# Differences in the comparison of the transform matrices: GpSimd in place of VectorE

## The chip, the cores and the metric

The kernel runs on one core of a Trainium2 chip. Its engines each work through a list of their own: TensorE (PE; PEld is its loading of weights), VectorE (DVE), ScalarE (ACT), GpSimd (POOL) and SyncE (SP), which here issues the transfers (DMA). They meet at semaphores only. The metric is the device time of one execution in microseconds (us). The time before is a median of 1157.23 us over three runs (1155.76 to 1159.63).

## What is computed

The reference adds two branches to its input, both fed by the same layer norm (S = 2048 rows, D = 512):

```python
xn = layernorm(x)
# A: Fourier mixing with the transform matrices given as inputs
a = xn @ dft_hid_re.T;  b = xn @ dft_hid_im.T
A = dft_seq_re @ a - dft_seq_im @ b
# B: product-key experts: 32 heads, 64 x 64 keys, 4096 experts, top 2 each
q1, q2 = split(xn @ w_q);  s1, s2 = q1 @ k1.T, q2 @ k2.T
top_s, top_e = top2(top2(s1) + top2(s2));  g = softmax(top_s)
B = sum(g * gelu(xn . u[top_e]) * v[top_e])
out = x + A + B
```

The transform matrices are inputs, not constants. They normally have the symmetries of a Fourier transform: columns that are mirrored, or equal up to a sign. The kernel computes branch A from a part of each matrix, using these symmetries. So that the result holds for any input, it also reads the matrices as a whole and measures how far they are from the symmetries. A flag at the end selects a general branch where they are not; with these inputs it isn't taken.

## The kernel before, in words

**Stages.** Up to about 480 us the kernel normalizes, computes branch A by folded matrices, and routes branch B (scores, top values, indices). The rest, from about 480 us to the end, is the expert stage in `part_b`. It walks over 16 blocks of 128 rows. For a block b it has

- a **z phase**: for all 4096 experts, z = u . xn, by `u_part` (L975, 12 matmuls per group of 128 experts). ScalarE takes z from PSUM through gelu into the tile act (L982). Two blocks share a phase for most of the kernel, with z groups in four PSUM banks in turn.
- **g products** (`g_mm`): the routing weights as a dense matrix. VectorE builds one-hot matrices L (L1003) and R (L1008, then times the gate in L1011) for 16 rows at a time, in three buffers; TensorE multiplies them into PSUM (L1013), two halves of 16 rows per call.
- **w parts** (`w_part`): VectorE multiplies act by g (L1021, g is read from PSUM), ScalarE rounds it to f16 (L1028; VectorE does so in L1026 in the z phases), VectorE forms the remainder (L1029). Four parts make the block's left-hand side, in place in the act tile (which is called act or w in the trace).
- a **v phase**: `v_part` multiplies by v (L1058, 96 matmuls of 512 columns). Of 16 tiles of v nine stay in SBUF; seven are streamed from DRAM by SP (L1049), three buffers.
- `add_x` loads y (branch A's result) and x and adds them on GpSimd (L1071); `finish` adds the v sum (L1075) and stores (L1076).

The phases run z(2,3), v1, v2, z(4,5), v3, v4 and so on. So a v block with an odd number is followed by an even one, for which the last w part is made during the odd block; an even v block is followed by a z phase. While v of the even block runs, the g products and first w parts of the following odd block are made.

**The comparison.** 64 units `compare(n)` (L1080 to L1134) and four `compare_w(n)` measure the symmetries. A dictionary `plan` names after which group of a phase a unit is emitted: three units in each v block up to 13, at groups 4, 5 and 6, and five in each double z phase. A unit n takes a tile cx of 128 x 1024 f32 (four slots of 256 columns): the first 128 columns come with one transfer (L1087), the other 896 with another (L1088). Then

1. L1089 (VectorE) sums the absolute values of the first 128 columns.
2. Where g is 1, 2 or 3 (48 units), L1108 subtracts slot 0 from, or adds it to, the slots 1 to 3, in one instruction of 768 columns or in two of 512 and 256. Where g is 0 (16 units), slot 1 is done by L1095, slots 2 and 3 by two L1097 with a factor of 0 for partition 0, and L1099 does partition 0 of slot 3.
3. `mirror` (L1114, for kk = 0 also L1116) subtracts or adds mirrored halves, for the whole tile in slot 0, and where g is 0 for partition 0 in slot 2. L1128 adds a constant on partition 0 in four units; L1122, L1125, L1130 and L1133 set some entries to others or to zero.
4. ScalarE sums the absolute values of all that is left (L1134). This is put on the list `later`, so that it is emitted about two units later.

The tile cx comes from the pool tag "w" with four buffers (WB = 4), the same that the w parts use and that `fit` (sums over other weights, L1186, L1193, L1197) loads into.

**What sets the order.** The code is emitted in the order of the plan. A scheduler in the framework then makes one list for each engine when the program is built: it takes instructions by priority, with an estimate of its own of when their inputs are there, and places the waits. So the engine on which an instruction runs can shift the order of others on VectorE and ScalarE. Once built, the lists are fixed, and each engine works strictly in order.

Of the kernel before, what the change touches and what calls it, by code (L numbers as in the profile page):

```python
# [15 lines left out]
ALU = mybir.AluOpType  # L16
AX = mybir.AxisListType

P = 128
# [15 lines left out]
def tile_fnet_peer(ctx, tc, x, ca, cb, c5, wt, wf, wr, wq, kt, ut, vn, out):  # L35
# [9 lines left out]
    nc = tc.nc  # L45
# [494 lines left out]
    c52 = cst.tile([1, 2], F32, name="c52")  # L540
# [122 lines left out]
    def part_b(safe, stS, stP, stE, xt, u_sb, cmp_p, w4):  # L663
# [416 lines left out]
        def compare(n):  # L1080

            ri, g, kk = n // 32, n // 8 % 4, n % 8
            odd = kk // 4
            t = bp.tile([P, 4, 4, 64], F32, tag="w", name=f"cx{n}", bufs=WB)
            tf = t.rearrange("p s q c -> p (s q c)")
            tv = t.rearrange("p s q c -> p s (q c)")
            nc.sync.dma_start(tf[:, :P], ca[ri, g, :, kk * P:(kk + 1) * P])  # L1087
            nc.sync.dma_start(tf[:, P:], cb[ri, g, kk].rearrange("p b c -> p (b c)"))  # L1088
            nc.vector.tensor_reduce(asum[:, n:n + 1], tf[:, :P], axis=AX.X, op=ALU.add,  # L1089
                                    apply_absolute_value=True)  # L1090
            sgn = (((1, 1, 1), (-1, 1, -1)), ((-1, -1, 1), (1, -1, -1)))[ri][odd]
            ops = [ALU.subtract if v > 0 else ALU.add for v in sgn]
            op = ops[1]
            if g == 0:
                nc.vector.tensor_tensor(tv[:, 1], tv[:, 1], tv[:, 0], op=ops[0])  # L1095
                for i in (2, 3):
                    nc.vector.scalar_tensor_tensor(tv[:, i], tv[:, 0], not0, tv[:, i], op0=ALU.mult, op1=ops[i - 1])  # L1097
                f = (-1 if ri else 1) * sgn[1] * sgn[2]
                nc.vector.tensor_tensor(tv[0:1, 3], tv[0:1, 3], tv[0:1, 2],  # L1099
                                        op=ALU.subtract if f > 0 else ALU.add)  # L1100
            else:
                sets = {}
                for i, o in enumerate(ops):
                    sets.setdefault(o, []).append(i + 1)
                for o, ix in sets.items():
                    sl = slice(ix[0], ix[-1] + 1, ix[1] - ix[0] if len(ix) > 1 else 1)
                    v = tv[:, sl]
                    nc.vector.tensor_tensor(v, v, tv[:, 0:1].to_broadcast([P, len(ix), 256]), op=o)  # L1108
            m = ALU.add if ri else ALU.subtract

            def mirror(v):

                c = 0 if kk else 1
                nc.vector.tensor_tensor(v[:, 2:4, c:], v[:, 2:4, c:], v[:, 0:2, c:], op=m)  # L1114
                if c:
                    nc.vector.tensor_tensor(v[:, 3, 0:1], v[:, 3, 0:1], v[:, 2, 0:1], op=m)  # L1116

            if g == 0:
                mirror(t[0:1, 2])
                if odd and ri:  # L1120

                    nc.vector.tensor_copy(t[0:1, 2, 0:2], t[0:1, 0, 0:2])  # L1122
                elif odd == ri:
                    if ri:
                        nc.vector.memset(t[0:1, 2, 0:2], 0.0)  # L1125
                    else:
                        v = t[0:1, 2, 0:2].rearrange("p q (c a) -> p (q c) a", a=2)
                        nc.vector.tensor_tensor(v, v, c52.unsqueeze(1).to_broadcast([1, 64, 2]), op=ALU.add)  # L1128
                    if kk == 0:
                        nc.vector.memset(t[0:1, 2, 2, 0:1], 0.0)  # L1130
            mirror(t[:, 0])
            if kk == 0:
                nc.vector.memset(t[:, 0, 2, 0:1], 0.0)  # L1133
            later.append(lambda: nc.scalar.activation(tf[:, P:], tf[:, P:], AF.Abs, accum_out=chk[:, n:n + 1]))  # L1134
# [248 lines left out]
    with tc.If(rv > 0):  # L1383
        with tc.tile_pool(name="gen", bufs=1) as gp, \
# [10 lines left out]
            def gload(src, shape, tag, name):  # L1395
                t = gp.tile(shape, F32, tag=tag, name=name, bufs=2)
                nc.sync.dma_start(t, src)
                return t
# [6 lines left out]
            for q in range(4):  # L1405
                ya = gp.tile([P, 4, D], F32, tag="ya", name=f"gya{q}")
                for ri in range(2):
# [25 lines left out]
                    for a in range(4):  # L1433
# [12 lines left out]
                        o = gload(out[b * P:(b + 1) * P], [P, D], "o", f"go{b}")  # L1446
# [54 lines left out]
```

## Time and profile before

| | |
|---|---|
| median of three runs | 1157.23 us (1155.76 to 1159.63) |
| the profiled execution | 1159.15 us, its span 1157.3 us |
| TensorE busy | 1131.3 us (98%), mean granted clock 0.99 |
| VectorE busy | 930.0 us (80%) |
| ScalarE busy | 608.5 us (53%) |
| GpSimd busy | 256.3 us (22%), most of it before 480 us |
| DMA | 167.82 MB, mean 145 GB/s |
| comparisons | L1108 runs from 568.9 to 1018.4 us, L1114 from 501.0 to 1019.1 us |

How to read it: all rows of the profile are of one execution, in us from the start of its span. A group row names line, engine, operation, output tile <- input tiles, shapes and count; then busy time in us and the mean duration in ns; then the idle time of the engine just before these instructions and what ended it ("<-DMA cx" is a transfer into cx, "<-PE g L1013" a TensorE instruction). A row of waits has the total, the number and the longest wait. A row of the timeline has start, duration, engine and line. Matmuls are pipelined, so that the duration of one is longer than its share of the engine's time. GpSimd's spans are rough.

### The profile page before, as it was taken

The numbers are of one execution on the slowest core, as the hardware profiler recorded it, in microseconds if no ns is written. First come the engines' busy times: TensorE is split into PE (matmuls) and PEld (weight loads), VectorE is DVE, ScalarE is ACT, GpSimd is POOL, SyncE is SP. The second block draws the span as 40 slices with busy tenths as digits, with TensorE's granted clock in tenths as the row PEclk, the third lists the DMA queues.
The fourth block names the chain that finished last, engine by engine and source line by source line (L and its number), as shares of the span: only waits on it lengthen the run. The fifth ranks groups of instructions, "written<-read, shape, count | busy, mean of one in ns | idle before, by whom it ended". The sixth has DMA issues, their size and how long they took to land.

```text
span 1157.3 us, 25208 instructions
## 1 busy us (share of the span) xinstructions
PE 1131.3 (98%) x9862; PEld 719.8 (62%) x9862; DVE 930.0 (80%) x2846; ACT 608.5 (53%) x1045; POOL 256.3 (22%) x226
## 2 busy tenths in 40 slices
PE   5999899999999999999999999999999999999997
PEld 4445455445445459778478479569569559658763
DVE  7979789799898998974994895897886886788670
ACT  7765487686786735354435435535535436433440
POOL 2371464865865411000000000010010000000000
PEclk9998899999999999999999999999999999999999
DMA  9992345243241204261743743654555555452423
GB/s 344 229 254 90 129 132 176 63 163 128 74 164 47 83 15 125 84 213 38 245 148 105 233 163 107 220 162 137 185 159 174 169 172 168 156 167 63 138 75 104
DMA packets 98335, 167.82 MB, mean 145 GB/s; under 512 B 32916, under 2 KB 48155, under 8 KB 98206
## 3 DMA queue, kind: packets, MB, share of 16 engines
q1 hardware_dynamic: 97904, 166.04, 44.5%
q8 instruction: 79, 1.29, 0.5%
q14 instruction: 50, 0.41, 0.1%
q10 hardware_dynamic: 302, 0.08, 0.0%
HBM read 142.69 MB, written 17.63 MB: 139 GB/s over the span
## 4 chain that ended last, share of the span: by engine, by line
PE 63%; DVE 21%; POOL 7%; issue 3%; ACT 3%; DMA 2%; SPq 0%; POOLq 0%; DVEq 0%; ACTq 0%
PE v L1058 28%; PE z L975 26%; DVE vals L841 5%; PE s L245 5%; DVE idx L845 4%; PE g L1013 4%; POOL w L153 2%; POOL w L154 2%; POOL u L722 1%; DVE z L782 1%; DVE L L1003 1%; DVE m L220 1%; DVE ft L406 1%; DVE z L783 1%; DVE u L510 1%
## 5 line engine op out<-in xcount | busy, mean ns | idle before, releaser
L975 PE MATMUL z<-xb,u 128*128 128x256 f16 (+1 forms) x3840 | 342.7, 251 | 0.2 <-ACT w L982 0.2
L975 PEld LDWEIGHTS <-u 128*128 128x128 f16 x3840 | 309.7, 98 | 26.7 <-issue 0.3
L245 PE MATMUL s<-m,xq 128*128 128x512 f16 x1344 | 301.4, 383 | 0.0
L1058 PE MATMUL v<-v,act 128*128 128x512 f16 x1056 | 233.2, 379 | 0.0
L245 PEld LDWEIGHTS <-xq 128*128 128x128 f16 x1344 | 131.0, 99 | 155.0 <-issue 7.0
L1003 DVE TENSOR_TENSOR L<-io_lam,cmp 128x2048 f16<-128x2048 f16 x128 | 156.0, 1219 | 62.2 <-PE g L1013 62.1
L1058 PEld LDWEIGHTS <-act 128*128 128x128 f16 x1056 | 101.3, 98 | 117.6
L1071 POOL TENSOR_TENSOR y<-y,xr 128x512 f32<-128x512 f32 x15 | 28.1, 1874 | 612.9 <-DMA y<-y_d 393.1
L841 DVE MAX8 vals<-ss 128x8 f32<-128x64 f32 x896 | 133.6, 216 | 2.7 <-ACT ss L837 2.5
L982 ACT ACTIVATE act<-z,scl 128x256 f32<-128x256 f32 (+1 forms) x152 | 72.7, 502 | 119.4 <-PE z L975 119.3
L837 ACT ACTIVATE ss<-s,wsc 128x512 f32<-128x512 f32 x120 | 80.7, 682 | 57.5 <-PE s L245 50.4
L1058 PE MATMUL v<-v,w 128*128 128x512 f16 x480 | 106.2, 379 | 0.0
L1134 ACT ACTIVATE cx<-cx 128x896 f32<-128x896 f32 x64 | 60.4, 945 | 68.5 <-DVE cx L1114 47.3
L845 DVE FIND_INDEX8 idx<-vals,ss 128x8 uint16<-128x256 f32 x224 | 93.8, 419 | 0.0
L1028 ACT ACTIVATE act<-w 128x1024 f16<-128x1024 f32 x36 | 48.3, 1358 | 62.6 <-DVE w L1021 62.1
L1058 PEld LDWEIGHTS <-w 128*128 128x128 f16 x480 | 46.0, 98 | 53.4
L154 POOL TENSOR_TENSOR w<-w,wh 128x1024 f16<-128x1024 f32 x28 | 70.7, 2530 | 19.0 <-ACT w L151 18.0
L1021 DVE SCALAR_TENSOR_TENSOR w<-act,scl,g 128x1024 f32<-128x1024 f32 x44 | 55.7, 1275 | 19.8 <-ACT act L982 19.8
L1108 DVE TENSOR_TENSOR cx<-cx 128x512 f32<-128x512 f32 (+2 forms) x84 | 48.5, 612 | 24.8 <-DMA cx<-in_cb_dram 18.3
L1013 PEld LDWEIGHTS <-L 128*128 128x128 f16 x2048 | 60.7, 96 | 11.7 <-DVE R L1011 1.3
L1011 DVE TENSOR_TENSOR R<-R,cmp 128x512 f16<-128x512 f16 x128 | 61.5, 480 | 1.5
L1013 PE MATMUL g<-R,L 128*128 128x32 f16 x2048 | 61.8, 176 | 0.7 <-DVE R L1011 0.6
(298 smaller groups left out, 1310.9 us busy)
## 6 DMA issues: line engine op xcount, KB each, us to landing
v<-v_d SPq DMA_DIRECT2D x67, 512.0 KB, 4.2
cx<-in_cb_dram SPq DMA_DIRECT2D x64, 448.0 KB, 4.2
w<-in_wq_dram SPq DMA_DIRECT2D x28, 512.0 KB, 5.5
fit<-in_wq_dram SPq DMA_DIRECT2D x28, 512.0 KB, 4.6
uv<-in_vn_dram SPq DMA_DIRECT2D x16, 512.0 KB, 3.8
uv<-in_ut_dram SPq DMA_DIRECT2D x16, 512.0 KB, 6.8
c<-in_ca_dram SPq DMA_DIRECT2D x8, 512.0 KB
y<-y_d SPq DMA_DIRECT2D x16, 256.0 KB, 2.6
```

Source lines behind the costliest of these rows:

```text
L154: nc.gpsimd.tensor_tensor(l, raw, h, op=ALU.subtract)
L245: nc.tensor.matmul(ps, xt[i][:, l, kd, :], m[:, r, kd, :], start=(n == 0), stop=(n == 3 * KD - 1))
L837: nc.scalar.activation(s, ps, AF.Copy, scale=inv)
L841: nc.vector.max(vals[:, i, w, :, h], s[:, g, :])
L845: nc.vector.max_index(idx[:, i, w].rearrange("p k h -> p (k h)"), vals[:, i, w, 0:2].rearrange("p k h -> p (k h)"), s[:, w * HC:g + 1, :]. ...
L975: nc.tensor.matmul(ps if n == 1 else ps.rearrange("p (b n) -> p b n", b=2), ug[:, l, c % 2, kd, :], xb2[:, k0, r, kd, :] if n == 1 else xb ...
L982: nc.scalar.activation(ACT[bb][:, cg * m:cg * m + m, :], pv[:, i], AF.Gelu_apprx_tanh, scale=zsc)
L1003: nc.vector.tensor_tensor(L.rearrange("p t (l two) -> p t l two", two=2), io_lam.rearrange("p (l two) -> p l two", two=2).unsqueeze(1).to_ ...
L1011: nc.vector.tensor_tensor(Rv, Rv, bc(2, NC), op=ALU.mult)
L1013: nc.tensor.matmul(p[:, hf, t * NC:(t + 1) * NC], L[:, t, :], R[:, t, :], start=True, stop=True)
L1058: nc.tensor.matmul(pv, w16[:, c, :, l], v_sb[g][:, r, cc, :], start=(n + cc == 0 and k == 0), stop=(n == 15 and cc == 1 and k == 2))
L1134: later.append(lambda: nc.scalar.activation(tf[:, P:], tf[:, P:], AF.Abs, accum_out=chk[:, n:n + 1]))
```

## The change

The tensor_tensor instructions of `compare` go from `nc.vector` to `nc.gpsimd`: L1095, L1099, L1108, L1114, L1116 and L1128, with the same operands. VectorE keeps L1089, the L1097 with a factor per partition, and the copy and settings of L1122, L1125, L1130 and L1133; ScalarE keeps L1134. `compare_w` is unchanged.

```diff
             if g == 0:
-                nc.vector.tensor_tensor(tv[:, 1], tv[:, 1], tv[:, 0], op=ops[0])
+                nc.gpsimd.tensor_tensor(tv[:, 1], tv[:, 1], tv[:, 0], op=ops[0])
                 for i in (2, 3):
                     nc.vector.scalar_tensor_tensor(tv[:, i], tv[:, 0], not0, tv[:, i], op0=ALU.mult, op1=ops[i - 1])
                 f = (-1 if ri else 1) * sgn[1] * sgn[2]
-                nc.vector.tensor_tensor(tv[0:1, 3], tv[0:1, 3], tv[0:1, 2],
+                nc.gpsimd.tensor_tensor(tv[0:1, 3], tv[0:1, 3], tv[0:1, 2],
                                         op=ALU.subtract if f > 0 else ALU.add)
...
-                    nc.vector.tensor_tensor(v, v, tv[:, 0:1].to_broadcast([P, len(ix), 256]), op=o)
+                    nc.gpsimd.tensor_tensor(v, v, tv[:, 0:1].to_broadcast([P, len(ix), 256]), op=o)
...
-                nc.vector.tensor_tensor(v[:, 2:4, c:], v[:, 2:4, c:], v[:, 0:2, c:], op=m)
+                nc.gpsimd.tensor_tensor(v[:, 2:4, c:], v[:, 2:4, c:], v[:, 0:2, c:], op=m)
                 if c:
-                    nc.vector.tensor_tensor(v[:, 3, 0:1], v[:, 3, 0:1], v[:, 2, 0:1], op=m)
+                    nc.gpsimd.tensor_tensor(v[:, 3, 0:1], v[:, 3, 0:1], v[:, 2, 0:1], op=m)
...
-                        nc.vector.tensor_tensor(v, v, c52.unsqueeze(1).to_broadcast([1, 64, 2]), op=ALU.add)
+                        nc.gpsimd.tensor_tensor(v, v, c52.unsqueeze(1).to_broadcast([1, 64, 2]), op=ALU.add)
```

## Prediction

> **What bounds the kernel now.** I read the page's busy times and clock row first, then the busy time of the stage in which the comparisons run, then the waits of that stage.
>
> ```profile
> PE 1131.3 (98%) x9862; PEld 719.8 (62%) x9862; DVE 930.0 (80%) x2846; ACT 608.5 (53%) x1045; POOL 256.3 (22%) x226
> PEclk9998899999999999999999999999999999999999
> 500.00:1040.00 540.00, 540.00 (x4997) 377.57 (x4996) 418.71 (x740) 250.75 (x469) 20.72 (x12) 1.00 0.50 163
> 1100.00:1158.00 58.00, 51.09 (x435) 28.14 (x432) 22.93 (x45) 13.56 (x19) 0.70 (x1) 0.98 0.27 88
> ```
>
> The stretch rows give length, then busy us of PE, PEld, DVE, ACT and POOL, then the granted clock. From 500 to 1040 us, where every comparison runs, TensorE is busy 540.00 of 540 us at full clock. VectorE has 121 us free there, GpSimd 519 us. So VectorE is not the bound, and relief on it buys nothing by itself; it would pay only where TensorE waits for it.
>
> ```profile
> ACT cx L1134 <- DVE cx L1114: 47.3, 20, 5.6
> DVE L L1003 <- PE g L1013: 42.1, 18, 9.0
> PE z L975 <- ACT w L982: 0.2, 1, 0.2
> ```
>
> These are waits between 495 and 1100 us (total, times, longest). TensorE waits 0.2 us in all. VectorE itself waits 42.1 us for TensorE to give L and R buffers back. ScalarE waits 47.3 us for comparisons already, and TensorE does not feel it. **The best that this change can do for the stage is 0.2 us.** What it can do is make TensorE wait.
>
> **What is removed from VectorE.** The groups between 495 and 1100 us (line, operation, count, busy us, mean ns):
>
> ```profile
> L1108 DVE TENSOR_TENSOR cx<-cx 128x512 f32<-128x512 f32 (+2 forms) x84 | 48.5, 612 | 24.8 <-DMA cx<-in_cb_dram 18.3 <-ACT act L982 2.5 <-ACT w L982 2.2
> L1114 DVE TENSOR_TENSOR cx<-cx 128x128 f32<-128x128 f32 (+1 forms) x80 | 21.6, 284 | 0.8
> L1095 DVE TENSOR_TENSOR cx<-cx 128x256 f32<-128x256 f32 x16 | 6.6, 414 | 6.6 <-DMA cx<-in_cb_dram 5.5 <-ACT cx L1134 0.9 <-issue 0.3
> L1099 DVE TENSOR_TENSOR cx<-cx 1x256 f32<-1x256 f32 x16 | 6.5, 408 | 0.2
> L1116 DVE TENSOR_TENSOR cx<-cx 128x1 f32<-128x1 f32 (+1 forms) x10 | 1.3, 146 | 0.0
> L1128 DVE TENSOR_TENSOR cx<-cx,c 1x128 f32<-1x128 f32 x4 | 1.1, 274 | 0.0
> ```
>
> 48.5 + 21.6 + 6.6 + 6.5 + 1.3 + 1.1 = 85.6 us and 210 instructions leave VectorE. GpSimd's list in the changed program is longer by the same 210, so the change does what it says. The order of TensorE's and SP's instructions is the same as before; VectorE's and ScalarE's orders shift.
>
> **What is added to GpSimd.** The trace has GpSimd's tensor_tensor in several sizes; the third row is the y addition (shortest, median and longest duration), the last has L1108's forms.
>
> ```profile
> L795 POOL TENSOR_TENSOR di<-if 128x128 f32<-128x128 f32 x7 | 3.2, 458 | 0.1
> L790 POOL TENSOR_TENSOR if<-if,hoff 128x256 f32<-128x256 f32 x7 | 4.3, 614 | 3.5 <-DVE if L787 3.5
> L1071 POOL TENSOR_TENSOR y<-y,xr x15: 1262/1576/3903, 457.6 to 1096.2; 128x512 f32<-128x512 f32 x15
> L1108 DVE TENSOR_TENSOR cx<-cx x84: 406/683/983, 568.9 to 1018.4; 128x512 f32<-128x512 f32 x36, 128x256 f32<-128x256 f32 x36, 128x768 f32<-128x768 f32 x12
> ```
>
> 458 ns for 128 columns and 1262 ns for 512 make 2.1 ns per column and 190 ns fixed: 0.7 us for 256 (the row with a repeated operand says 0.61) and 1.8 us for 768. L1108: 36 x 1.26 + 36 x 0.7 + 12 x 1.8 = 92 us. L1114: 80 x 0.46 = 37. L1095 and L1099: 32 x 0.7 = 22. L1116 and L1128: an estimate of 3. Together **154 us undisturbed**, into 519 us of free time: GpSimd doesn't become the bound. If every one is stretched as the longest L1071 is, by 3903/1262, it is 476 us, still inside.
>
> The Trainium skill (GPSIMD Engine Reference, "Elementwise — side-by-side cycle accounting") gives 1.96 times VectorE's time for a two-input f32 addition. By that, 85.6 us become an estimated 168 us instead of 154, and nothing else moves.
>
> **What the two engines do to each other.** Three places in the timeline, in order of start (start, duration):
>
> ```profile
> 576.19 2.37 DVE L1029 TENSOR_TENSOR act<-w,act 128x1024 f16<-128x1024 f32 x1
> 594.28 1.25 DVE L1003 TENSOR_TENSOR L<-io_lam,cmp 128x2048 f16<-128x2048 f16 x1
> 594.53 2.46 POOL L1071 TENSOR_TENSOR y<-y,xr 128x512 f32<-128x512 f32 x1 [17.18 <-DVE act L1029]
> 595.41 0.46 DVE L1008 TENSOR_TENSOR R<-io_c,cmp 128x512 f16<-128x512 f16 x1
> 595.90 1.38 DVE L1011 TENSOR_TENSOR R<-R,cmp 128x512 f16<-128x512 f16 x1
> 663.25 1.27 DVE L1021 SCALAR_TENSOR_TENSOR w<-w,scl,g 128x1024 f32<-128x1024 f32 x1
> 663.38 1.27 POOL L1071 TENSOR_TENSOR y<-y,xr 128x512 f32<-128x512 f32 x1 [66.38 <-DVE R L1008]
> ```
>
> At 594.53 GpSimd's addition takes 2.46 us instead of 1.26: it gets through only after L1003 and L1008, and then L1011, elsewhere 0.41 to 0.49 us, takes 1.38 and ends when the addition does. L1029 at 576.19 took 2.37 us against 1.3. Beside L1021, whose g comes from PSUM, the addition ran its plain 1.27 us and L1021 lost nothing. So a VectorE instruction with two SBUF inputs and a GpSimd tensor_tensor take turns, each for a whole instruction.
>
> The Trainium skill (SBUF — State Buffer, "Who interferes with whom") says this as a rule: whichever starts first holds the shared read interface and the other blocks fully. The trace agrees (1.38 against 0.42 us).
>
> What VectorE pays is bounded by 0 and by all 154 us. The instructions that must take turns:
>
> ```profile
> L1003 DVE TENSOR_TENSOR L<-io_lam,cmp 128x2048 f16<-128x2048 f16 x106 | 129.2, 1219 | 42.2 <-PE g L1013 42.1
> L1011 DVE TENSOR_TENSOR R<-R,cmp 128x512 f16<-128x512 f16 x107 | 51.7, 483 | 1.4
> L1008 DVE TENSOR_TENSOR R<-io_c,cmp 128x512 f16<-128x512 f16 x107 | 44.8, 419 | 0.0
> L1029 DVE TENSOR_TENSOR act<-w,act 128x1024 f16<-128x1024 f32 x33 | 44.6, 1352 | 1.0 <-ACT act L1028 0.9
> L1029 DVE TENSOR_TENSOR w<-w,w 128x1024 f16<-128x1024 f32 x20 | 26.0, 1298 | 0.5 <-ACT w L1028 0.5
> L1097 DVE SCALAR_TENSOR_TENSOR cx<-cx,not 128x256 f32<-128x256 f32 x32 | 14.9, 505 | 0.0
> ```
>
> They sum to 311 of 605 us, 51%. Taking half of GpSimd's time as blocked, VectorE gives up 85.6 us and pays about 79. Its load stays near 419 - 86 + 79 = 412 of 540 us; with the full 154 it is 487. **On average nothing is bound; the price is local**, where a chain through GpSimd has less slack than it gains delay.
>
> **Place 1: the end of an even v block.** The last g product of the block waits on VectorE's R, which stands behind L1029, which waits for ScalarE's L1028. Block 4, before:
>
> ```profile
> 667.68 1.03 DVE L1108 TENSOR_TENSOR cx<-cx 128x512 f32<-128x512 f32 x2 [0.24 <-DMA cx<-in_cb_dram]
> 670.33 1.37 ACT L1028 ACTIVATE w<-w 128x1024 f16<-128x1024 f32 x1
> 671.73 1.32 DVE L1029 TENSOR_TENSOR w<-w,w 128x1024 f16<-128x1024 f32 x1
> 675.85 0.44 DVE L1011 TENSOR_TENSOR R<-R,cmp 128x512 f16<-128x512 f16 x1
> 678.31 0.95 PE L1013 MATMUL g<-R,L 128*128 128x32 f16 x32
> ```
>
> R is ready at 676.3, TensorE needs it for the second half of its 32 matmuls at about 678.7: slack 2.4 us. In the changed order, for blocks 2, 4, 8 and 10, ScalarE has the sums of absolute values (L1134) of both comparisons ahead of that L1028. Data land at 667.7. First comparison: 1.26, then the blocked L1011 and L1003 go between (0.4 + 1.2), then 0.7 + 0.46 beside L1021: 671.7. Second: 1.26, L1008 and L1003 between (1.6), 0.7 + 0.46: 675.7. L1134 0.95 and its read 0.19, L1028 1.37, L1029 1.3, L1011 0.43: R at 680.0, **1.3 us late**. Without any turns lost (2 x 2.42 from 667.7) it is 676.9, 1.8 early; with 1.3 us more per instruction (2.46 is 1.2 over plain, 3.90 is 2.6), some 8 late. Blocks 2 and 8 have the 768-column form or a later landing; in block 6 VectorE's L1097 waits for GpSimd instead. I take 1.5 us for each of these five ends: 7.5 us.
>
> **Place 2: the end of an odd v block.** The last L1029 must end before the next block's first v matmul, just before L1075's 656.27:
>
> ```profile
> 651.88 1.34 DVE L1029 TENSOR_TENSOR act<-w,act 128x1024 f16<-128x1024 f32 x1
> 656.27 0.75 DVE L1075 SCALAR_TENSOR_TENSOR y<-v,scl,y 128x512 f32<-128x512 f32 x1 [0.48 <-PE v L1058]
> ```
>
> Slack: 656.0 - 653.2 = 2.8 us. Ahead stand one L1134 (its comparison later by 1.8 less L1108's longest 0.98 on VectorE, and about 1 for turns) and up to 1.3 us of blocking on L1029: 1.8 to 3.1 us against 2.8, so 0 to 1.5 us each; 0.5 for six such ends: 3 us.
>
> **Costed at nothing.** ScalarE's L1134 in the z phases stands ahead of L982; the work that hides it is two to three more z groups in other PSUM banks. SP is held when a buffer of the w pool comes free later, with v loads queued behind its comparison loads. VectorE's L1097 and L1133 now wait for GpSimd; the relief of 85.6 us covers them. GpSimd's own y additions queue behind comparisons, a whole block ahead of their use. If these covers go, the next rival's price applies.
>
> **Sum.** 7.5 + 3 = 10.5, say +10 us on the profiled execution's 1159.15 us (span 1157.3 and 1.85 around it): 1169. That execution lay 1.9 us above the median 1157.23, so the prediction is **1167 us**, own range 1161 to 1178.
>
> **The rivals.** *Absorbed (not slower), 1157:* GpSimd starts a comparison when its data land instead of in VectorE's queue, and finds L1021 or idle VectorE each time. It decides where R's delay stays under 1.7 to 2.4 us at place 1; the 1.8 us early end of my bound and the 1.27 us row speak for it, the 2.46 and 3.90 us rows against. Chance 0.22. *Cascade, about 1192:* GpSimd is starved as in the 3.90 us row, the ends of even blocks pay 5 x 5 us and the odd ones 6 x 1.5, w buffers and SP's loads slip: +35. VectorE's long unbroken runs speak for it, its 22% idle time against. Chance 0.10. *Faster, 1155:* relief on VectorE would have to shorten a wait of TensorE; there is 0.2 us in the stage, and the 7 us idle after 1100 come after the comparisons. 0.06.
>
> **How the numbers follow.** Forecast 0.62, absorbed 0.22, cascade 0.10, faster 0.06. About 0.3% (3.5 us) is what a measurement of this kernel can tell from no change: slower 0.62 + 0.10 = 0.72, same 0.22, faster 0.06. The range goes from the absorbed case to the lower part of the cascade: 1156 to 1190.
>
> **What would show it.** GpSimd busy 150 to 250 us more; VectorE between 500 and 1040 within 40 us of 419; mean of L1011 and L1029 up; new TensorE waits of 1 to 3 us on R at L1013 and on L1029 at L1058, at block ends and nowhere else. It is wrong if TensorE still waits under 1 us in the stage, or if the waits sit at z on L982 or v on DMA.

## The result, and the profile after

The changed kernel takes **1174.96 us** (median of 4 runs, 1173.68 to 1177.38), the kernel before 1158.43 us in the same comparison (4 runs, 1155.76 to 1160.39): ratio 1.0144, 95% interval 1.0129 to 1.0159. So it is **slower by 1.4%**, 16.5 us. The profiled execution took 1173.68 us, its span 1171.7 us against 1157.3 before.

Three parts of the profile after answer to those shown of before. First the busy times and the clock row of the page:

```profile
PE 1136.4 (97%) x9862; PEld 721.9 (62%) x9862; DVE 908.8 (78%) x2636; ACT 605.8 (52%) x1045; POOL 453.1 (39%) x436
PEclk9999999999999999999999999999999999999999
```

Then the stretch of the comparisons, and three short stretches inside it (length, busy us of PE, PEld, DVE, ACT and POOL, granted clock, share of DMA, GB/s):

```profile
500.00:1040.00 540.00, 530.17 (x4849) 370.54 (x4847) 380.56 (x491) 243.93 (x462) 217.35 (x216) 0.99 0.48 158
680.00:690.00 10.00, 9.65 (x86) 7.99 (x86) 9.37 (x13) 2.41 (x5) 2.34 (x1) 0.83 0.21 64
810.00:820.00 10.00, 8.22 (x78) 7.03 (x79) 6.19 (x11) 4.51 (x12) 0.00 (x0) 0.83 0.01 2
870.00:880.00 10.00, 10.00 (x107) 8.58 (x106) 8.56 (x11) 3.25 (x7) 2.60 (x1) 0.87 0.36 99
```

TensorE was busy 540.00 of 540 us at clock 1.00; now 9.8 us of that stretch are idle, and in three places the granted clock falls. The page's clock row is too coarse to show it: in slices of 29 us a stretch of a few us at half clock is lost. Third, the waits between 495 and 1100 us:

```profile
POOL cx L1108 <- DMA cx<-in_cb_dram: 144.6, 27, 24.0
ACT cx L1134 <- POOL cx L1114: 126.9, 43, 6.9
DVE L L1003 <- PE g L1013: 37.1, 14, 10.3
PE g L1013 <- DVE R L1011: 8.9, 7, 3.0
DVE act L1029 <- ACT act L1028: 6.1, 7, 2.6
PE z L975 <- ACT act L982: 1.3, 2, 1.1
```

GpSimd is idle for its data most of the time, so it is no bound. But ScalarE's L1134, which waited 47.3 us for VectorE's L1114, now waits 126.9 us for GpSimd's, and TensorE has waits on R that it did not have.

**Where the time went.** I take the start of the first matmul of each phase and compare the phases with those before. From z(2,3) to the start of v13 the changed kernel loses 17.2 us: 6.7 in the even v blocks (blocks 2, 4, 6, 8, 10, 12: 0.49, 2.13, 0.35, 2.41, 0.00, 1.36), 0.00 in the odd ones, 1.5 in z(2,3), 8.5 in the five double z phases after it (0.19, 1.67, 4.32, 1.67, 0.66) and 0.4 in z14. It had been 2.7 us ahead at 500 us, mostly since two half-clock stretches (stretches with a granted clock of 0.50) near 90 and 128 us were 3.41 us long instead of 6.83; this belongs to the start of the program. 17.2 - 2.7 is the difference of the spans, 14.4 us, but for 0.1.

In block 4 the mechanism stands in the timeline (start, duration, engine, line; the row order is that of time):

```profile
669.32 2.13 POOL L1108 TENSOR_TENSOR cx<-cx 128x512 f32<-128x512 f32 x2 [0.72 <-DMA cx<-in_cb_dram]
669.56 1.31 DVE L1011 TENSOR_TENSOR R<-R,cmp 128x512 f16<-128x512 f16 x1
672.82 2.14 POOL L1108 TENSOR_TENSOR cx<-cx 128x512 f32<-128x512 f32 x2
672.88 0.95 ACT L1134 ACTIVATE cx<-cx 128x896 f32<-128x896 f32 x1 [6.72 <-POOL cx L1114]
676.39 0.95 ACT L1134 ACTIVATE cx<-cx 128x896 f32<-128x896 f32 x1 [2.46 <-POOL cx L1114]
677.34 1.34 ACT L1028 ACTIVATE w<-w 128x1024 f16<-128x1024 f32 x1
678.71 1.28 DVE L1029 TENSOR_TENSOR w<-w,w 128x1024 f16<-128x1024 f32 x1 [2.67 <-ACT w L1028]
679.89 0.41 DVE L1011 TENSOR_TENSOR R<-R,cmp 128x512 f16<-128x512 f16 x1
680.35 0.55 PE L1013 MATMUL g<-R,L 128*128 128x32 f16 x16 [1.98 <-DVE R L1011]
```

The two comparisons run on GpSimd one after the other and take turns with VectorE (7.1 us together, from 669.32 to the second L1134, against 4.8 us undisturbed). Both L1134 wait for them, L1028 stands behind both, L1029 and R behind L1028, and TensorE stands still for 1.98 us. R ended at 680.30; the prediction had worked out 680.0.

ScalarE's list differs from before here. In the kernel before, L1028 ran at 670.33, between the two L1134 of block 4:

```profile
669.18 0.95 ACT L1134 ACTIVATE cx<-cx 128x896 f32<-128x896 f32 x1 [3.26 <-DVE cx L1114]
671.85 0.95 ACT L1134 ACTIVATE cx<-cx 128x896 f32<-128x896 f32 x1 [0.16 <-DVE cx L1114]
```

In blocks 2, 4, 8 and 10 the scheduler has put the second L1134 ahead of L1028 in the changed kernel. Right behind the first one, L1028 could have started at 673.9 instead of 677.34. VectorE was busy until 676.0, so R would have come some 2.4 us earlier, an estimate from these times; the gap is 1.98.

In z(8,9), where the five units have g = 0, the same kind of chain has more steps:

```profile
805.57 1.35 DVE L1097 SCALAR_TENSOR_TENSOR cx<-cx,not 128x256 f32<-128x256 f32 x2 [2.05 <-DMA cx<-in_cb_dram]
808.58 0.21 DVE L1122 COPY cx<-cx 1x128 f32<-1x128 f32 x1 [1.65 <-POOL cx L1114]
808.72 1.20 DVE L1003 TENSOR_TENSOR L<-io_lam,cmp 128x2048 f16<-128x2048 f16 x1
811.32 0.41 DVE L1011 TENSOR_TENSOR R<-R,cmp 128x512 f16<-128x512 f16 x1
811.78 0.59 PE L1013 MATMUL g<-R,L 128*128 128x32 f16 x16 [3.04 <-DVE R L1011]
```

VectorE, in order, waits 2.05 us for a late transfer into cx and 1.65 us for GpSimd's mirror before it may go on to L and R.

### The profile page after: what moved, and what is told of

The parts are those of the page before. It is cut to its first block, busy times and chain, and to the rows that moved or that the text cites. A ratio compares the mean times of both kernels' runs of the same rounds, so it can differ in the third digit from the quotient of the medians.

```text
span 1171.7 us, 25328 instructions
## 1 busy us (share of the span) xinstructions
PE 1136.4 (97%) x9862; PEld 721.9 (62%) x9862; DVE 908.8 (78%) x2636; ACT 605.8 (52%) x1045; POOL 453.1 (39%) x436
## 4 chain that ended last, share of the span: by engine, by line
PE 65%; DVE 15%; DMA 8%; POOL 6%; ACT 3%; issue 3%; SPq 1%; POOLq 0%; DVEq 0%; ACTq 0%
PE s L245 24%; PE z L975 20%; PE v L1058 16%; DMA cx<-in_cb_dram 5%; PE g L1013 3%; POOL cx L1108 3%; DVE L L1003 2%; PE m L135 1%; POOL cx L1114 1%; DVE u L841 1%; DVE w L1021 1%; DVE act L1029 1%; ACT cx L1134 1%; DVE u L845 1%; DVE R L1008 1%
## 5 line engine op out<-in xcount | busy, mean ns | idle before, releaser
L975 PE MATMUL z<-xb,u 128*128 128x256 f16 (+1 forms) x3840 | 347.8, 253 | 2.1 <-ACT act L982 1.3
L1003 DVE TENSOR_TENSOR L<-io_lam,cmp 128x2048 f16<-128x2048 f16 x128 | 168.5, 1317 | 60.8 <-PE g L1013 56.6
L1108 POOL TENSOR_TENSOR cx<-cx 128x512 f32<-128x512 f32 (+2 forms) x84 | 112.5, 1356 | 160.6 <-DMA cx<-in_cb_dram 144.6
L1134 ACT ACTIVATE cx<-cx 128x896 f32<-128x896 f32 x64 | 60.8, 950 | 152.8 <-POOL cx L1114 126.9
L982 ACT ACTIVATE act<-z,scl 128x256 f32<-128x256 f32 (+1 forms) x152 | 72.4, 504 | 87.1 <-PE z L975 87.1
L1071 POOL TENSOR_TENSOR y<-y,xr 128x512 f32<-128x512 f32 x15 | 31.0, 2068 | 141.3 <-DMA y<-y_d 73.6
L1011 DVE TENSOR_TENSOR R<-R,cmp 128x512 f16<-128x512 f16 x128 | 78.5, 614 | 1.7
L1028 ACT ACTIVATE act<-w 128x1024 f16<-128x1024 f32 x36 | 48.1, 1353 | 54.7 <-DVE w L1021 54.5
```

The costliest lines, as they stand in the source:

```text
L975: nc.tensor.matmul(ps if n == 1 else ps.rearrange("p (b n) -> p b n", b=2), ug[:, l, c % 2, kd, :], xb2[:, k0, r, kd, :] if n == 1 else xb ...
L982: nc.scalar.activation(ACT[bb][:, cg * m:cg * m + m, :], pv[:, i], AF.Gelu_apprx_tanh, scale=zsc)
L1003: nc.vector.tensor_tensor(L.rearrange("p t (l two) -> p t l two", two=2), io_lam.rearrange("p (l two) -> p l two", two=2).unsqueeze(1).to_ ...
L1011: nc.vector.tensor_tensor(Rv, Rv, bc(2, NC), op=ALU.mult)
L1108: nc.gpsimd.tensor_tensor(v, v, tv[:, 0:1].to_broadcast([P, len(ix), 256]), op=o)
```

## The experiments

**How to read them.** The theory that I set out with: the loss is made by comparisons whose results come late, in front of other work on ScalarE (L1028, L982), on SP (the loads into w buffers) and on VectorE (L1122). The rivals: VectorE and GpSimd block each other, and this alone costs the time (load); or late buffers alone do it (buffers). The table has, for the profiled run of each kernel, what its phases lose against before (us, from the first matmuls of the phases), how many half-clock stretches of 3.41 us lie between 495 and 1100 us (what they cost is inside the columns before, but for the one after block 12 with the rounding on VectorE: z14 loses 1.2 us there), and the ratio of the medians with its interval.

| kernel | z(2,3) | six even v blocks | z(4,5) to z(12,13) | half-clock | median us | ratio to before |
|---|---|---|---|---|---|---|
| changed | 1.5 | 6.7 | 8.5 | 3 | 1174.96 | 1.0144 (1.0129 to 1.0159) |
| only g = 0 on GpSimd | 2.0 | 0.0 | 2.5 | 0 | 1162.46 | 1.0049 (1.0035 to 1.0062) |
| only g = 1, 2, 3 | 0.0 | 6.3 | 4.8 | 1 | 1168.69 | 1.0095 (1.0078 to 1.0113) |
| w part 1 rounded on VectorE | 1.6 | 3.0 | 6.4 | 1 | 1171.04 | 1.0123 (1.0108 to 1.0138) |
| five buffers | 1.8 | 9.8 | 3.1 | 3 | 1167.05 | 1.0077 (1.0064 to 1.0090) |
| both of these | 1.9 | 4.5 | 0.0 | 1 | 1161.97 | 1.0031 (1.0018 to 1.0043) |
| both, only g = 1, 2, 3 | 0.0 | 1.7 | 0.0 | 0 | 1158.89 | 0.9999 (0.9989 to 1.0009) |
| before, five buffers | 0.0 | 0.0 | 0.0 | 0 | 1159.79 | 1.0007 (0.9998 to 1.0016) |
| before, and blocking | 0.0 | 7.7 | 0.0 | 0 | 1166.53 | 1.0067 (1.0051 to 1.0083) |
| blocking with relief | 0.0 | 0.0 | 0.0 | 0 | 1158.55 | 0.9994 (0.9985 to 1.0004) |
| more blocking, relief | 0.0 | 0.0 | 0.0 | 0 | 1158.49 | 1.0005 (0.9996 to 1.0014) |
| one input on GpSimd | 1.6 | 2.7 | 8.1 | 1 | 1168.92 | 1.0091 (1.0060 to 1.0122) |

The changed kernel and its variants spread more than before (five buffers: 1165.32 to 1173.22, and the profiled run is the longest), so a column of one profile says where time went, and the ratio how much.

### Which units

```diff
-                    nc.gpsimd.tensor_tensor(v, v, tv[:, 0:1].to_broadcast([P, len(ix), 256]), op=o)
+                    nc.vector.tensor_tensor(v, v, tv[:, 0:1].to_broadcast([P, len(ix), 256]), op=o)
...
-                nc.gpsimd.tensor_tensor(v[:, 2:4, c:], v[:, 2:4, c:], v[:, 0:2, c:], op=m)
+                (nc.gpsimd if g == 0 else nc.vector).tensor_tensor(v[:, 2:4, c:], v[:, 2:4, c:], v[:, 0:2, c:], op=m)
...
```

> Only the 16 units with g = 0 compare on GpSimd (L1095, L1099, L1128 and their L1114 and L1116); the 48 others stay on VectorE. Theory (late chains): the changed kernel loses 17 us after 500 us in three separate terms: 6.7 us at the ends of the even v blocks, 4.5 us in three half-clock stretches that follow its longest TensorE gaps, and the rest in z(2,3) and z(8,9), where the units with g = 0 go to and fro between GpSimd and VectorE. So here z(2,3) +1.5 and z(8,9) +4.3 (with its half-clock stretch), the ends of blocks 2 to 12 under 0.5 us each: 5 to 7 us more than before, about 1164 us. Rival (load): GpSimd blocks VectorE wherever it runs, and the loss goes with its busy time; these units are some 45 of the 197 us added: 3.8 us, spread over the phases. Rival (buffers): the loss comes from the late release of the four w buffers, with whichever unit: then the loss is in the phases that hold these units, but with waits on DMA, not on R.

Measured: 4.5 us over before. z(2,3) loses 2.0 and z(8,9) 2.5, all else nothing, as the theory had it; the gap in z(8,9) is there, but no half-clock stretch follows it (see the clock, below), so the sum is below the 5 to 7 us that were expected.

The second is the opposite: L1095, L1099 and L1128 back on `nc.vector`, `(nc.gpsimd if g else nc.vector)` for the mirror.

> Only the 48 units with g = 1, 2 or 3 compare on GpSimd (L1108 and their L1114 and L1116); those with g = 0 stay on VectorE. Theory (late chains): ends of the even blocks about 6.7 us, two half-clock stretches after blocks 4 and 8 about 3.3 us, z(8,9) and z(2,3) under 0.5 us each: 9 to 11 us more than before, about 1168 us. Rival (load): 150 of the 197 us added on GpSimd: 12.5 us, z(8,9) and z(2,3) at zero too but the loss in all the other phases. Rival (buffers): as the load, with TensorE waits on DMA.

Measured: 10.7 us over before, in the range, and z(2,3) and z(8,9) at 0.00. The inside is not as told: block 8 loses 4.2 us (a 1.1 us wait on a tile of v besides 2.7 us on R), blocks 2 and 6 nothing, and z(6,7) loses 1.9 us, most of it in one wait of z on ScalarE's L982, with no half-clock stretch. The two sets add up to 15.2 of the 16.5 us. The losses of z(2,3) and z(8,9) belong to the units with g = 0, those at the ends of the v blocks to the others.

### Which queue

```diff
-                put(ph, 7, W(b + 1, 1), G(b + 1, 2))
+                put(ph, 7, W(b + 1, 1, True), G(b + 1, 2))
```

> All as in the changed kernel, but the w part 1 of the odd blocks, made at the end of the even v blocks, is rounded on VectorE (L1026) and not on ScalarE (L1028): it no longer stands in ScalarE's list behind the two L1134 that wait for GpSimd. Theory (late chains): in block 4, L1028 was ready at 673.7 and ran at 677.3, so R comes 3.6 us earlier, less 0.7 for L1026: the gaps at the ends of blocks 4, 8 and 12 go (4.9 us of the 6.7), and the half-clock stretches after 4 and 8 with them (3.3 us): 7 to 9 us less than the changed kernel, about 1167 us; z(8,9) stays at +4.3. Rival (load): VectorE gets 6 x 0.7 us more work and is as blocked as before: 1174 to 1179, the gaps stay. Rival (buffers): no change, 1175.

Measured: 3.9 us less than the changed kernel, half of what was expected. The ends of blocks 2 to 10 lose 0.00 each: with L1028 out of ScalarE's list, R is in time, though VectorE does more and is blocked as before (L1011's mean is 667 ns). So at these ends the wait behind L1134 is necessary for the loss. But block 12 now loses 3.0 us, with a half-clock stretch after it, and z(6,7) and z(10,11) lose 1.4 us each where the stretches had been. In block 12 units of `compare_w` (VectorE, unchanged) and the added L1026 stand ahead of the last R; that this is its cause is read from the timeline and not tried.

```diff
-        WB = 4
+        WB = 5
```

> All as in the changed kernel, with five w buffers instead of four. Theory (late chains): at the ends of the even blocks L1021 did not wait for a buffer, so the gaps of blocks 4 and 8 and their half-clock stretches stay; in z(8,9) the loads into cx come earlier, so that its 3 us gap may shrink: 0 to 5 us less than the changed kernel, 1170 to 1175 us. Rival (buffers): all of the loss goes, 1157 to 1161 us. Rival (load): no change, 1175.

Measured: 7.9 us less than the changed kernel, between the theory and the rival. z(8,9) loses 0.00 instead of 4.32. The ends of blocks 4 and 8 keep their gaps and half-clock stretches, and block 2 gets a new loss: 2.3 us on a transfer of v, with a half-clock stretch. SP's waits tell how the buffers work: its comparison loads (L1087) wait for L1134 to free a w buffer. The same row of before, of the changed kernel, and with five buffers (total, times, longest):

```profile
SPq L1087 <- ACT cx L1134: 32.0, 12, 5.3
```

```profile
SPq L1087 <- ACT cx L1134: 65.6, 20, 5.8
```

```profile
SPq L1087 <- ACT cx L1134: 1.8, 1, 1.8
```

A comparison that ends late frees its buffer late, the next load starts late, and the next comparison is late from its start. The fifth buffer cuts this circle.

The next has both edits, the rounding up to block 11 (`W(b + 1, 1, b < 12)`):

> The changed kernel with both chains shortened: five w buffers, and w part 1 of the odd blocks up to 11 rounded on VectorE (L1026). Theory: the rounding took the gaps at the ends of blocks 4 and 8 and their half-clock stretches (8 us in the profiled runs), the fifth buffer the 4.3 us of z(8,9) and the loss in z(6,7); what is left is z(2,3) with 1.5 to 2 us and perhaps the wait on v's transfer that came up in block 2 with five buffers (4.5 us with its half-clock stretch): 1160 to 1165 us. Rival (VectorE and GpSimd block each other wherever they meet, and the loss only changes its place): 1167 us or more.

Measured: 3.7 us over before, as the theory had it. All ends but block 2's are at 0.24 or less, all double z phases after z(2,3) at 0.00, although GpSimd compares all 64 units and VectorE is as blocked as in the changed kernel (L1011's mean is 651 ns against 654). The rival falls. What is left is z(2,3) and, in the profiled run, block 2.

> The kernel before with five w buffers instead of four. Two runs of the changed kernel with five buffers lost 4.3 to 4.5 us in block 2, where TensorE waited for a tile of v and a half-clock stretch followed. Theory: SP runs further ahead with comparison loads, whichever engine compares, and the transfer of v comes late: the same 2 to 4.5 us here, 1160 to 1163 us. Rival: the wait on v needs GpSimd's comparisons too: no change, 1157 to 1159 us.

Measured: no change. The theory's half of this one fell: five buffers alone don't delay v in block 2.

> Only the 48 units with g = 1, 2 or 3 on GpSimd, and both chains shortened as in the run before (five w buffers, w part 1 rounded on VectorE up to 11). Theory: the 1.9 us that z(2,3) lost there come from the units with g = 0 and go; what is left is the wait on v in block 2 (2 to 4.5 us, if it is there): 1158 to 1162 us, with z(4,5) to z(12,13) and the ends of the even blocks at zero. Rival (VectorE and GpSimd block each other wherever they meet): 48 of the 64 units remain, so two thirds or more of the loss of any version: 1165 us.

Measured: 0.9999, no difference to before. With 48 of 64 units on GpSimd and both chains shortened nothing is lost in z(2,3), and one wait on v is left (1.7 us, block 8). The loss in z(2,3) comes from the units with g = 0 on GpSimd; every kernel that has them there loses 1.5 to 2 us in it, five buffers or four. In the changed kernel one wait makes 1.09 of the 1.54 us:

```profile
515.38 1.45 POOL L1071 TENSOR_TENSOR y<-y,xr 128x512 f32<-128x512 f32 x1
516.79 0.71 POOL L1099 TENSOR_TENSOR cx<-cx 1x256 f32<-1x256 f32 x1
518.37 0.95 ACT L1134 ACTIVATE cx<-cx 128x896 f32<-128x896 f32 x1 [2.76 <-POOL cx L1114]
520.18 3.98 PE L975 MATMUL z<-xb,u 128*128 128x256 f16 x35 [1.09 <-ACT act L982]
```

GpSimd's y addition stands between two steps of a comparison, L1134 waits 2.76 us for the last step, L982 stands behind L1134, and TensorE finds no free bank. No run takes L1071 alone away, so this is read, not shown.

### Blocking or lateness

Here the comparison stays on VectorE, and GpSimd does the same work on a tile of its own:

```diff
-        later = []
+        later = []; dum = bp.tile([P, 768], F32, tag="dum", name="dum", bufs=1); nc.gpsimd.memset(dum, 0.0)
...
-                                    apply_absolute_value=True)
+                                    apply_absolute_value=True); [nc.gpsimd.tensor_tensor(dum[:, :N], dum[:, :N], asum[:, n:n + 1].to_broadcast([P, N]), op=ALU.mult) for N in ((256, 256, 128) if g == 0 else (512, 256, 128))]
```

> The kernel before, with all comparisons on VectorE, and beside them the same amount of work on GpSimd that nobody waits for: after each L1089 three tensor_tensor of 512, 256 and 128 columns (256, 256 and 128 where g is 0) on a tile of its own, with the sum of L1089 as the second input. GpSimd's results are not used. It blocks VectorE as in the changed kernel, and adds no step to the chain of a comparison. Theory (late chains: the loss needs a comparison's result that comes late, in front of something on ScalarE or SP): VectorE's instructions get longer (L1011 from 483 ns to above 600), but R is still in time at most block ends: 0 to 4 us more than before, 1158 to 1162 us. Rival (blocking alone is enough): VectorE carries 85 us more than in the changed kernel and is blocked as much, so at least the changed kernel's loss: 1172 us or more.

Measured: 8.3 us over before, between the two. Each even block loses 1.1 to 1.5 us, waiting for R, and no z phase anything:

```profile
PE g L1013 <- DVE R L1011: 6.6, 7, 1.4
PE z L975 <- ACT w L982: 0.7, 1, 0.7
```

So blocking alone does cost, where VectorE has all its work besides (busy 458.47 us between 500 and 1040, before 418.71). It makes VectorE's own comparisons late too: L1134 waits 68.4 us for L1114, before 47.3. In the changed kernel VectorE has 85.6 us less. The next run gives it that: the six lines on `nc.vector` are replaced by `pass`, and L1134 gets `scale=0.0`.

> As the run with blocking alone (the same work on a tile of its own on GpSimd, which nobody waits for), and in addition VectorE's six lines of comparison (L1095, L1099, L1108, L1114, L1116, L1128) are left out, and L1134 multiplies by 0: the comparison is not computed. So VectorE has the relief and the blocking of the changed kernel, and no result of GpSimd is waited for. Theory (the gaps at the ends of the even blocks need both the blocking and a late L1134 ahead of L1028): no gaps over 0.5 us, 0 to 2 us more than before: 1158 to 1160 us. Rival (blocking alone stretches the end of each even block by 1.1 to 1.5 us, as it did with VectorE fully loaded): six such gaps again, 1164 to 1167 us.

Measured: 0.9994, and 0.00 in every phase from z(2,3) on but z14 (0.35). But its blocking was weaker, so it was run once more with `(320, 320, 152, 152)` and `(640, 320, 152)` columns:

> As the run with blocking and relief (comparison left out on VectorE, work on a tile of its own on GpSimd), with GpSimd's instructions made longer: 640, 320 and 152 columns instead of 512, 256 and 128, and four where g is 0. In the run before, GpSimd's 512 columns took 1.04 us, in the changed kernel 1.27 us, and it was busy 154 us more than before against 197; L1011 came to 581 ns against 651. Now GpSimd's time should reach that of the changed kernel, about 190 us more, and L1011 620 to 660 ns. Theory (blocking by itself costs nothing as long as VectorE has the relief and no result is late): no gap over 0.5 us, 1157 to 1160 us. Rival (the run before was free only because its blocking was weaker): gaps at the ends of the even blocks again, 1163 us or more.

Measured: 1.0005. The stretch row stands beside that of the changed kernel above: GpSimd 213.36 us busy against 217.35, VectorE 390.32 against 380.56, and TensorE 540.00 of 540:

```profile
500.00:1040.00 540.00, 540.00 (x4984) 377.12 (x4982) 390.32 (x529) 250.87 (x469) 213.36 (x219) 1.00 0.50 164
```

L1011's mean came to 612 ns, a little below the 654 of the changed kernel. In blocks 2, 4, 8 and 10 both L1134 stand ahead of L1028 here as well, so that order alone does not make the loss either. **With the relief, blocking of this size cost nothing here; the loss needs a result that comes late.** The rival (load) falls for this kernel, with one reserve: GpSimd starts here when the first 128 columns are summed, not when the whole tile has landed, so the amount of blocking is matched and its places are not.

The other way round, with GpSimd in the chain and its blocking changed: `tensor_scalar(v, v, 0.0, None, op0=ALU.mult)` in place of each of GpSimd's tensor_tensor.

> The changed kernel, with GpSimd's tensor_tensor replaced by a tensor_scalar that multiplies the same columns in place by 0: the comparison itself is left out, GpSimd's instructions read one input instead of two. The chain (GpSimd, then ScalarE's L1134 and its place in the list) is that of the changed kernel. If one input takes no turns with VectorE, L1011 comes back to about 0.48 us and L1108 starts when its data land. Theory (late chains, made late by the turns): in block 4 R comes at about 677 instead of 680, in time; the gaps of the even blocks and their half-clock stretches go (11 us), and z(8,9) loses at most half of its 4.3: 1159 to 1164 us. Rival (the place of L1134 in ScalarE's list is enough, with GpSimd at its plain speed): the gaps of blocks 4 and 8 stay at 1 to 2 us each: 1168 us or more. If the instructions take turns all the same, 1170 to 1176.

Measured: 10.7 us over before, above the theory's range and inside the rival's. An instruction with one input takes turns too: L1011's mean is 541 ns, not 483. At the ends of blocks 2, 4 and 6 nothing is lost and at block 8 0.35, as the theory had it (in block 4 R is there at 678.3, 22.3 us after the start of the phase against 24.8 in the changed kernel), at block 10 1.7 and at block 12 0.6. But z(8,9) loses 3.6 and the z phases in all 9.7, with L1134 waiting for GpSimd even longer and TensorE for L982:

```profile
ACT cx L1134 <- POOL cx L1114: 144.2, 51, 6.9
PE z L975 <- ACT act L982: 5.2, 5, 1.8
```

So the two parts of the loss differ. The gaps at the ends of blocks 4 and 8 need L1134 ahead of L1028 (the rounding took them away, and turns alone, with the relief, make none). With one input they shrink to 0.00 and 0.35, but this does not show that the turns had made them: of the 2.5 us by which R is earlier in block 4, 2.0 come from a first comparison that starts earlier in the phase (11.8 instead of 13.8 us after its start) and only 0.5 from shorter comparisons; in block 8 it is 1.4 and 0.7. The loss of the z phases is as large with VectorE less blocked. There it goes with the late result: GpSimd's instructions with one input are slower by themselves (512 columns at least 1.48 us instead of 1.26). A GpSimd step that takes no turns at all could not be had from these instructions, so lateness quite without blocking was not measured.

### The clock

```diff
-                nc.vector.tensor_tensor(Rv, Rv, bc(2, NC), op=ALU.mult)
+                nc.vector.tensor_tensor(Rv, Rv, bc(2, NC), op=ALU.mult); [nc.vector.tensor_scalar(L, L, 1.0, None, op0=ALU.mult) for _ in range(DOSE.get(b, 0) if tg == 2 and hf else 0)]
```

Here `DOSE = {3: 4, 5: 5, 7: 6, 9: 7, 11: 8, 13: 9}`, in the kernel before.

> The kernel before with TensorE gaps made on purpose: at the ends of blocks 2, 4, 6, 8, 10 and 12 the last L of the next block's g product is multiplied by 1 on VectorE 4, 5, 6, 7, 8 and 9 times, so that TensorE waits for it. GpSimd does nothing more than before. Theory (a half-clock stretch of 3.41 us follows a window of 3.41 us of a fixed grid in which TensorE was idle for more than some 1.8 to 2.0 us): a half-clock stretch follows just those gaps that take 2 us or more out of one window, and none follows a shorter gap or a longer one that two windows share with less than 1.8 us in each; each stretch costs 1.7 us. Rival (the half clock comes from something else in the changed kernel, the power that GpSimd draws beside VectorE for one): no half-clock stretch here.

Measured, in one execution: 1179.08 us, and three half-clock stretches, at 776.04, 871.61 and 1062.76 us, with GpSimd doing no more than before. So the rival falls. Stretches on the 3.41 us grid, with TensorE's busy time in the second number:

```profile
772.62:776.04 3.42, 0.85 (x19) 0.55 (x18) 3.42 (x7) 0.00 (x0) 0.00 (x0) 1.00 0.20 77
776.04:779.45 3.41, 3.41 (x25) 2.44 (x22) 3.41 (x6) 1.00 (x3) 0.56 (x1) 0.50 0.21 77
963.77:967.18 3.41, 1.78 (x29) 1.46 (x28) 3.08 (x6) 0.95 (x2) 0.08 (x1) 1.00 0.28 84
967.18:970.60 3.42, 3.42 (x43) 3.08 (x42) 3.42 (x5) 0.96 (x3) 1.19 (x1) 1.00 0.26 80
```

After 0.85 us busy the clock halves for one step of the grid, after 1.78 it does not. The theory's limit was 2 us of idle time; the last section narrows it.

## Why the prediction was right, and where it was not

**Right as a whole**: slower was given 0.72, the range 1156 to 1190 and the own range 1161 to 1178 hold 1174.96. The loss was told as 10 us and measured as 16.5. The best that the change could do was put at 0.2 us; no run here is faster than before beyond its interval.

**What is added, right.** The groups after, on GpSimd and on VectorE:

```profile
L1108 POOL TENSOR_TENSOR cx<-cx 128x512 f32<-128x512 f32 (+2 forms) x84 | 112.5, 1356 | 160.6 <-DMA cx<-in_cb_dram 144.6 <-DMA cx<-in_ca_dram 6.8 <-ACT w L982 5.6
L1114 POOL TENSOR_TENSOR cx<-cx 128x128 f32<-128x128 f32 (+1 forms) x80 | 48.6, 613 | 3.8
L1095 POOL TENSOR_TENSOR cx<-cx 128x256 f32<-128x256 f32 x16 | 16.5, 1034 | 111.9 <-DMA cx<-in_cb_dram 107.0 <-ACT act L982 2.9 <-ACT cx L1134 2.0
L1099 POOL TENSOR_TENSOR cx<-cx 1x256 f32<-1x256 f32 x16 | 15.0, 935 | 12.4 <-DVE cx L1097 12.4
L1003 DVE TENSOR_TENSOR L<-io_lam,cmp 128x2048 f16<-128x2048 f16 x105 | 140.6, 1339 | 41.3 <-PE g L1013 37.1 <-ACT w L982 4.2
L1011 DVE TENSOR_TENSOR R<-R,cmp 128x512 f16<-128x512 f16 x106 | 69.3, 654 | 1.6
L1008 DVE TENSOR_TENSOR R<-io_c,cmp 128x512 f16<-128x512 f16 x105 | 57.6, 549 | 0.8 <-DVE w L1021 0.8
L1097 DVE SCALAR_TENSOR_TENSOR cx<-cx,not 128x256 f32<-128x256 f32 x32 | 21.4, 705 | 10.1 <-DMA cx<-in_cb_dram 7.3 <-ACT act L982 2.8
```

GpSimd is busy 453.1 - 256.3 = 197 us more: 154 undisturbed, most of the rest is waiting for turns inside its instructions; 150 to 250 was foretold. VectorE is at 380.56 us between 500 and 1040, within the 40 us of 419 that were given.

**What VectorE pays, too high.** L1003 rose by 120 ns, L1011 by 171, L1008 by 130 and L1097 by 200; by their counts 12.7 + 18.3 + 13.9 + 6.4 = 51, with L1029 (47 and 74 ns) 54 us. The prediction took half of GpSimd's time, 79. This changed nothing: VectorE did not become a bound either way. The longer instructions also show that the engines do not meet at semaphores only, as the opening has it: VectorE and GpSimd hold each other up inside instructions.

**Place 1, right in mechanism, its sum near in part by luck.** 7.5 us were given to five even ends (blocks 2, 4, 6, 8 and 10). These lost 5.4: blocks 4 and 8 were dearer than told (2.1 and 2.4), 2 and 6 cheaper, 10 free. Block 12, which had been given nothing, lost 1.4. In block 4 R came at 680.30, told 680.0, but the phase had begun 0.5 us earlier than before (655.50 against 655.99): R was 0.8 us later in the phase than told, and the gap 1.98 us instead of 1.3. Two errors partly cancel in it. GpSimd started the first comparison 13.8 us into the phase instead of 11.7, behind its y addition and a late transfer, and the two comparisons took 7.1 us instead of 8.0. The rounding run shows the queue that the step named, the wait behind L1134. That the turns make it late is read from the durations; no run takes away the turns alone. The "some 8 late" of the outer bound is a slip: six instructions longer by 1.3 us, from 1.8 early, make 6.

**Place 2, wrong by its whole size.** The odd ends were given 3 us, and each lost 0.00. The step's own terms, 1.8 to 3.1 us against a slack of 2.8, reach 0.3 us at most, not the 1.5 that it wrote. The slack between the last L1029 and the first v matmul was 2.6, 2.8, 1.7, 1.5, 2.3 and 2.9 us after the change (4.5, 2.8, 2.8, 4.4, 2.8 and 2.8 before): up to 2.9 us of it was used up and never all.

**"Costed at nothing", the step that failed.** The prediction held that L1134 ahead of L982 is hidden by "two to three more z groups in other PSUM banks", that VectorE's waits for GpSimd are covered by its relief, and that SP's held loads matter only in the cascade. The z phases lost 10.0 us of the 17.2 (1.5 and 8.5). Of this, 3.0 us are the gap in z(8,9), which the run with five buffers took away: SP's loads did slip, from 32.0 to 65.6 us of waits, short of a cascade. 1.5 us are z(2,3), where the PSUM cover gave out. And 4.6 us are a term that the prediction did not have at all: three half-clock stretches of 3.41 us behind TensorE's gaps at blocks 4 and 8 and in z(8,9). They cost about half their length, 1.67 and 1.67 us, and, where TensorE stood still for part of it, 1.28 us (z(8,9)'s 4.32 less the gap of 3.04, so at most that). The last 0.9 us are small waits in z(4,5) and z(12,13). "At block ends and nowhere else" was wrong for the same reason.

That the total was still near came from errors of both signs: 3 us too much at place 2, about 1 at the even ends, 10 too little in the z phases; 10.5 told against 17.2, of which the shorter start-up took 2.7 back in the profiled run.

**The rivals.** *Absorbed* is what the two runs with blocking and relief show: without a late result, 1158.5 us. Its condition, that R's delay stays inside the slack, held there; in the changed kernel it failed where L1028 stood behind late L1134. *Cascade* named one true place (w buffers and SP, 3.0 us in z(8,9)) and overpriced it. *Faster*: nothing.

**What stays open.** Why v's transfer comes late in block 2 with five buffers and the units with g = 0 on GpSimd (0.00 with either alone); the gap of block 12 with the rounding on VectorE; whether z(2,3) would be saved by moving L1071. Above all, no run has the comparison on GpSimd and ScalarE's list of before, with L1028 ahead of the second L1134. By the timeline of block 4 that would have saved the gap there. So how much of the loss at the even ends is the scheduler's new order, and how much GpSimd's time, is not separated.

## What to carry to other kernels

Moving work to an idle engine moves its result in time, and it can change the lists that the scheduler builds for the other engines; read both. Before asking whether the engines block each other, follow who reads the result: which instruction on a third engine waits for it, what stands behind that one in its list, which buffer it frees and which load waits for the buffer. A TensorE gap of 2 us can cost another 1.7 us through the clock where two of 1 us cost nothing more, so gaps are priced one by one, not as a sum.

## What the runs showed of the hardware

**Half clock after a gap that is shorter than a window.** The three half-clock stretches of the changed kernel begin at 681.36, 811.07 and 869.10 us: 38.0 and 17.0 times 3.413 us apart. I cut TensorE's time between 495 and 1100 us into such steps, in the profiles of all kernels here, each by the grid of its own clock changes. The clock halves after every step in which TensorE was idle for 1.81 us or more (13 steps, up to 3.41) and after none with 1.77 us or less. The two nearest steps to the limit, one input and only g = 1, 2, 3:

```profile
806.58:810.00 3.42, 1.61 (x29) 1.42 (x26) 3.33 (x5) 2.98 (x8) 0.40 (x1) 1.00 0.00 0
810.00:813.41 3.41, 3.41 (x18) 2.45 (x17) 0.46 (x2) 1.31 (x4) 0.00 (x0) 0.50 0.02 5
```

```profile
711.01:714.42 3.41, 1.64 (x16) 1.32 (x15) 3.41 (x3) 2.86 (x7) 2.89 (x2) 1.00 0.00 0
714.42:717.83 3.41, 3.41 (x59) 3.13 (x57) 1.70 (x3) 3.41 (x10) 0.00 (x0) 1.00 0.02 5
```

Busy 1.61 us of 3.41 is too little, 1.64 enough. And the gap of 2.4 us in z(8,9) of the kernel with only g = 0 cost no clock, since it was shared by two steps:

```profile
803.36:806.77 3.41, 2.35 (x34) 2.15 (x33) 1.90 (x4) 1.60 (x4) 1.48 (x3) 1.00 0.00 0
806.77:810.19 3.42, 2.12 (x32) 1.94 (x32) 3.39 (x6) 2.35 (x7) 0.00 (x0) 1.00 0.00 0
```

The place of a gap in the grid decides, and the grid is not tied to the kernel; this may be why variants with gaps of about 2 us spread more than the kernel before.

The Trainium skill (TensorE: Matmul & The Clock Gate, "Part 1: The HAM clock gate (the "warmup" mystery)") has the free-running window of 3413 ns, and the traces agree (3.41). It has the clock fall after an idle window; here a window with 1.81 us of idle time did it, and the measurement decides.

**One input is not quicker on GpSimd.** In the one-input run its 512 columns took a mean of 1652 ns, in the changed kernel 1417, both with turns. The Trainium skill (SBUF — State Buffer, "Who interferes with whom") says that a VectorE instruction with two SBUF inputs contends with a GpSimd instruction that reads SBUF; the run agrees (L1011 541 ns against 483).
